# A weight rounding rewritten with an integer addition, and small sums, pooling and maxima moved, in a fused attention and mixing kernel

## The chip, the cores and the metric

One Trainium2 chip, one core. The metric is the device time of one execution in microseconds (us), median of three runs; lower is better.

## What is computed

For each of 8 batches and 8 heads: 1152 keys of width 64, and 576 queries that are the means of two neighbours. Then softmax attention, and a second stage on its output `x` (8 x 576 x 512):

```python
q_pool = q.reshape(B, H, S // 2, 2, D).mean(axis=3)
scores = scale * q_pool @ k.T ; scores -= scores.max(-1)
x = (exp(scores) / (exp(scores).sum(-1) + 1e-9)) @ v
theta = x @ w_theta
y = w_tok_r @ (x * cos(theta)) + w_tok_i @ (x * sin(theta))
u = x + y
out = u + max(u @ w_ch, 0)
```

q, k and v are 32-bit floats. The four weight matrices come as 64-bit floats, two 32-bit words each, and the kernel narrows them itself.

## The kernel before

**Stage one** takes the heads in 32 pairs. A pair has 18 steps, which the code calls positions: two halves `u` of the queries, with 9 key tiles `kt` each. In a step `escore` (line 671) issues four kinds of products on TensorE (high and low parts, and one that subtracts the row maximum), and ScalarE takes the exponential of the result into a buffer `pc` (line 674), of which there are 14. GpSimd adds the buffers of a half up, `ssum` (line 686): for each half seven additions of 128 x 576 numbers, key tiles 0 to 7 (`TAIL = 8`). The ninth tile, `kt = 8`, is not added there. `norm_sum` (line 735) sums over the keys with products by a block of ones, and takes the buffers from `TAIL` on as further operands. It runs a whole pair later, just after the first burst of the next pair, so that such a buffer is held until then. For pairs in `WHOLE` (25 to 30) VectorE adds the ninth tile instead (`whole_sum`, line 754).

A **burst** (`av`, line 706) is the product with v: 36 matmul instructions that read the nine `pc` buffers of one half. It stands at positions 10.348 (first half) and 19.269 (second half, so 1.269 of the next pair). ScalarE then copies the result (`xu`, line 718) and the row of maxima (line 629).

Meanwhile the next pairs are prepared: `load_q` and `load_k` by DMA, `pool_q` (line 487), which adds neighbouring queries, some 2.8 pairs ahead, on VectorE for pairs in `POOL_V` (before: none) and else on GpSimd; 32 x 32 transposes on VectorE (lines 516 and 520), rounding to the high part on ScalarE (`round_hi`, line 528), and the low part on VectorE (`round_lo`, line 572). TensorE also computes a rough product for the row maxima two pairs ahead (`maxpass`, line 585), which VectorE reduces (lines 597 and 616).

**Weights.** Beside this runs a generator, `weights`, with 18 jobs: four blocks each of `w_theta` and `w_ch` (128 x 512), five each of the two token matrices (128 x 576, the last 64 x 576). Each `yield` names the kind of the next step, and the table `W_SLOTS` says at which positions of a pair a step of a kind may run: F fetches the next block, A is work of ScalarE, D of VectorE, G of GpSimd, S and T split the result into high and low parts (T with transposes on TensorE). A job takes one pair. In the pairs of `REST` the slots after position 10.3455 are left out, so that those pairs do only the head of a job. `narrow` makes a 32-bit float from the two words: line 814 takes the absolute value of the high word, 815 scales the low word, 817 and 819 clamp and shift on VectorE, 824 puts the sign back, 828 masks the exponent, 830 multiplies it with the scaled low word on GpSimd, and 832 adds both there.

**Order.** The order of each engine's instructions is written out: every call goes on a list with a position and a priority (`at`, `plan`), which is then sorted; nothing is reordered afterwards. `PLAN`, `MAX_A`, `MAX_B` and `ROUND_AT` hold positions relative to the pair that is prepared; `SS_LAG` is how far an addition of line 686 stands behind its exponential.

```python
PC_BUFS = 14
at(base + KT * u + kt, 1, escore, i, u, kt)
at(base + KT * u + kt + (SS_LAG if i < NPAIR - 1 else 1.2), 8, ssum, i, u, kt)
at(base + (AV_AT if i else AV_AT0)[u], 4, burst, i, u)
```

**Stage two** (lines 1092, 1139 and 324 on TensorE) follows from about 865 us on and is not touched by the change.

Of the kernel before, what the change touches and what calls it, by code (L numbers as in the profile page):

```python
# [10 lines left out]
F32 = mybir.dt.float32  # L11
F32R = mybir.dt.float32r
U32 = mybir.dt.uint32
I32 = mybir.dt.int32
AF = mybir.ActivationFunctionType
ALU = mybir.AluOpType
AX = mybir.AxisListType

EPS = 1e-9
TAIL = 8  # L20
REST = (3, 6, 9, 12, 15, 18)
WHOLE = range(25, 31)
WARM = 16
AGAIN = ((3, 3, 3, 3, 3, 3, 3, 3, 3, 5, 3, 3), (3, 2, 1, 1, 1, 1, 1, 1, 1, 1, 1, 1))
PC_BUFS = 14
MAX_A = ((-23.79, -21.22, -20.37, -19.03, -18.14, -16.75), (-22.88, -21.22, -20.11, -19.13, -18.62, -17.88))
MAX_B = ((-14.28, -12.84, -11.93, -9.1, -7.7, -7.7), (-14.26, -12.84, -11.93, -9.1, -8.62, -7.7))
LATE = (4, 5, 10, 11, 16, 17, 21, 22, 23, 24, 26, 27)
G_FROM = 20
G_AT = 3.43  # L30
SS_LAG = 6.71
AV_AT = (10.348, 19.269)
AV_AT0 = (10.348, 19.269)
W_SLOTS = ((2.5139, 'F'), (2.5144, 'G'), (3.4324, 'G'), (10.3436, 'S'), (10.3441, 'G'), (10.3446, 'T'), (10.3451, 'A'), (11.0187, 'D'), (11.0192, 'D'), (14.1909, 'F'), (17.9513, 'D'), (17.9518, 'D'))
W_STORE = 14.5
W_SLOTS0 = ((12.6, "F"),)
POOL_V = ()
ROUND1 = (-21.9, -21.8, -21.7)
LOADV = (-58.9, 11)
TAIL_IN = (3, 2)  # L40
# [11 lines left out]
NM_AT = (0.2, 13)  # L52
ROW_AT = (0.7, 13)
PLAN = {
    "load_q": -67.965,
    "load_k": -51.9564,
    "pool_q": -50.015,
    "turn_q": -34.8283,
    "turn_k": -34.0064,
    "tail": -25.3624,  # L60
    "round_lo": -25.1995,
    "load_max": -7.6,
    "load_v": -6.3045,
    "max_nm": -7.69,
    "norm_spread": 29.0,
    "norm_store": 20.81,
}
MAN = ("PE", "Activation", "DVE", "Pool", "SP")
RING = 4
# [35 lines left out]
OT_LAST = "htmmr"  # L105
CH_LAST = ("mr", "mr", "mm", "mh")
CH_BANK = "mrmr"
ROUND_AT = (-26.599, -26.599, -25.976)
XN_LEAD = 7.918
XF_LAG = 0.627  # L110
XS_LAG = 0.27
TINY = 2.0**-15
MAGIC = 12582912.0
INV2PI = 1.0 / (2.0 * math.pi)
C1 = 6.28125
C2 = 2.0 * math.pi - C1
# [5 lines left out]
def pooled_attention_moe_kernel(  # L122
# [11 lines left out]
    nc = tc.nc  # L134
    P = 128
    B, H, S, D = k.shape
    SQ = S // 2
# [4 lines left out]
    KT = S // P  # L142
# [22 lines left out]
    magic = const.tile([P, 1], F32, name="magic")  # L165
    nc.vector.memset(magic, MAGIC)
    halfpi = const.tile([P, 1], F32, name="halfpi")
# [21 lines left out]
    def done(name):  # L189
        slots.append(held.pop(name))  # L190
# [138 lines left out]
    def chain(b, j):  # L329
# [16 lines left out]
        if b == 0 and j == 0:  # L346
            pools["kk"] = kk
        nc.scalar.activation(kk, th, AF.Identity, bias=magic, scale=INV2PI)
        yield
        nc.vector.tensor_scalar(kk, kk, -MAGIC, None, ALU.add)  # L350
        r2 = tmp("r2")
# [62 lines left out]
    with ExitStack() as p1:  # L414
# [67 lines left out]
        def pool_q(i):  # L482
            qn = state[i]["qn"]
            qp = state[i]["qp"] = inp.tile([P, TB, 32], F32, tag="qp", name=f"qp{i}")
            eng = nc.vector if i in POOL_V else nc.gpsimd
            a, b = (qn.rearrange("p (m x) r -> p m x r", x=2)[:, :, x] for x in range(2))
# [190 lines left out]
        def ssum(i, u, kt):  # L677
            st = state[i]
            if i == NPAIR - 1:
                return last_sum(st, u, kt)  # L680
            if kt == 0 or kt >= TAIL:
                return
            if kt == 1:
                st["ss", u] = nrm.tile([P, 2, HALF], F32, tag=f"ss{u}", name=f"ss{u}_{i}", bufs=2)
            first = st["pc"][u, 0] if kt == 1 else st["ss", u]
            nc.gpsimd.tensor_tensor(st["ss", u], first, st["pc"][u, kt], ALU.add)  # L686

        def last_sum(st, u, kt):
            if kt < 2 or kt >= TAIL:
                return  # L690
# [32 lines left out]
        def norm_sum(i, px):  # L723
            st = state[i]
            last = i == NPAIR - 1
            sets = [
                ([st["sum", u, 0], st["sum", u, 1]] if last else [st["ss", u]])
                + [st["pc"][u, kt] for kt in range(TAIL, KT) if i not in WHOLE]
                for u in range(2)
            ]  # L730
            for n in range(len(sets[0])):
                for h in range(2):
                    for u in range(2):
                        a = 32 * (2 * h + u)
                        nc.tensor.matmul(  # L735
                            px[a : a + 32, 1, 0:HALF],
                            ones,
                            sets[u][n][:, h, :],
                            start=(n == 0),
                            stop=(n == len(sets[0]) - 1),  # L740
                            tile_position=(0, a),
                        )
            sm = st["sm"] = sml.tile([P, HALF], F32, tag="sm", name=f"sm{i}", bufs=1)
            if last:
                nc.vector.tensor_scalar(sm, px[:, 1, 0:HALF], EPS, None, ALU.add)
            else:
                nc.scalar.activation(sm, px[:, 1, 0:HALF], AF.Identity, bias=eps)
            done("pend" if last else f"pn{i + 1}")

        def whole_sum(i, u):  # L750
            if i in WHOLE:
                st = state[i]
                for kt in range(TAIL, KT):
                    nc.vector.tensor_tensor(st["ss", u], st["ss", u], st["pc"][u, kt], ALU.add)
# [28 lines left out]
        def weights():  # L783
            wst = pw.enter_context(tc.tile_pool(name="wst", bufs=1, side="right"))
            wide = w_theta.dtype != F32

            def words(w):
                if not wide:
# [11 lines left out]
            def narrow(raw, ws, R, n, g):  # L800
                dst = ws[0:R, 0:n].rearrange("a (t p) -> a p t", t=g)
                if not wide:
                    yield "D"
                    nc.vector.tensor_copy(
                        dst, raw[0:R, 0:n, 0].rearrange("a (p t) -> a p t", t=g)
                    )
                    yield "F"
                    return
                lo, hi = raw[0:R, 0:n, 0], raw[0:R, 0:n, 1]
                f = wst.tile([P, SQ], U32, tag="wf", name="wf")[0:R, 0:n]  # L810
                tl = lo.bitcast(F32)
                mk = ws[0:R, 0:n]
                yield "A"
                nc.scalar.activation(mk, hi.bitcast(F32), AF.Abs)
                nc.scalar.activation(tl, lo, AF.Copy, scale=2.0**-52)
                yield "D"
                nc.vector.tensor_scalar(mk, mk, TINY, None, ALU.max)
                yield "D"
                nc.vector.tensor_scalar(
                    f, mk.bitcast(U32), 3, 0x3FFFFFF8, ALU.logical_shift_left, ALU.bitwise_and  # L820
                )
                yield "F"
                yield "D"
                nc.vector.scalar_tensor_tensor(
                    f, hi, 0xC0000000, f, ALU.bitwise_and, ALU.bitwise_or
                )
                yield "D"
                nc.vector.tensor_scalar(hi, f, 0xFF800000, None, ALU.bitwise_and)
                yield "G"
                nc.gpsimd.tensor_tensor(tl, tl, hi.bitcast(F32), ALU.mult)  # L830
                yield "G"
                nc.gpsimd.tensor_tensor(
                    dst,
                    f.bitcast(F32).rearrange("a (p t) -> a p t", t=g),
                    tl.rearrange("a (p t) -> a p t", t=g),
                    ALU.add,
                )

# [119 lines left out]
        def plan(i):  # L958
# [15 lines left out]
            for n, (prio, fn) in fns.items():  # L974
                if n in EARLY.get(i, ()):
                    at(EARLY[i][n], prio, fn, i)
                elif i > 2 and n in pl:
                    at(base + pl[n], prio, fn, i)
            for n, t in enumerate(ROUND_AT if i > 2 else ()):
                at(base + t, 3, round_hi, i, n)  # L980
# [15 lines left out]
            for n in (MAX_AT0, MAX_AT1, MAX_AT2)[i] if i < 3 else (  # L996
                MAX_A[i - 2 in LATE] + MAX_B[i - 2 in LATE]
            ):
# [3 lines left out]
            for u in range(2):  # L1002
                for kt in range(KT):
                    at(base + KT * u + kt, 1, escore, i, u, kt)
                    at(base + KT * u + kt + (SS_LAG if i < NPAIR - 1 else 1.2), 8, ssum, i, u, kt)
            for u in range(2):
# [25 lines left out]
        for j in range(AHEAD):  # L1032
            t = NU * (NPAIR - 1) + TH_AT[j]
# [6 lines left out]
        for i in range(NPAIR):  # L1040
            at(NU * i + W_STORE, 11, wstore)
            for pos, kinds in W_SLOTS if i else W_SLOTS0:
                if i in REST and pos > 10.3455:
                    continue
                at(NU * i + (G_AT if pos == 5.0 and i >= G_FROM else pos), 10, wstep, kinds)
        for _, _, _, fn, args in sorted(todo, key=lambda e: e[:3]):
            fn(*args)

    with ExitStack() as p2:
# [157 lines left out]
        for b in range(B):  # L1207
            base = CYC * b
            if b > 0:
# [4 lines left out]
                for c in range(ND):  # L1214
                    at2(DN1_AT[c] if b == 1 else base + DN_AT[c], dload, b, c)
                    t = SC1_AT + 0.01 * c if b == 1 else base + SC_AT[c]
# [12 lines left out]
            for n, j in enumerate(TURNS[b % 2] if b else TURN0):  # L1229
                t = base + (THETA_AT if b % 2 == 0 else ODD_THETA_AT)[n] if b else THETA0_AT[n]  # L1230
# [15 lines left out]
            for g in range(2):  # L1246
                for i in range(KW):
                    at2(base + TOK_AT[g][i], token_mix, b, g, i)
                for c in (2 * g, 2 * g + 1):
                    t = base + PLAN2[f"uadd{g}"] + 0.7 * (c - 2 * g)  # L1250
# [7 lines left out]
            t = base + CH_AT[0]  # L1258
# [53 lines left out]
```

## Time and profile before

| | us |
|---|---|
| median of three runs (1306.94 to 1308.79) | 1308.12 |
| the profiled execution, whole | 1309.01 |
| its span, first to last instruction | 1307.2 |
| TensorE busy | 1252.2 |
| VectorE busy | 979.7 |
| GpSimd busy | 934.5 |
| ScalarE busy | 682.4 |

The span is the part that the trace shows; 1.8 us of the execution lie around it. PE is TensorE's matmuls, PEld its weight loads, DVE VectorE, ACT ScalarE, POOL GpSimd, SP the engine that issues DMAs. Busy time of PE is modelled and overlaps from one matmul to the next, so the length of a stretch is read from start to start. The burst of pair 0 starts at 37.82 us, that of pair 1 at 66.45, and the last pair's at 846.99; a pair's period is counted from first burst to first burst.

### The profile page before, as it was taken

What the parts mean: (1) busy time and instruction counts of PE and PEld (TensorE: products, weight loads), DVE (VectorE), ACT (ScalarE), POOL (GpSimd) and SP (SyncE); (2) the same over time, 40 slices, a digit from 0 to 9 for tenths busy, and PEclk for the clock granted to TensorE, in tenths of its full rate; (3) what the DMA queues carried; (4) which work ended last, traced back from release to release, by engine and by line L of the source; (5) the groups of instructions that cost most, each with busy time, mean ns of one, the idle gap of its engine ahead of it and who ended that gap; (6) DMA issues with size and microseconds to landing.
All of it is one profiled execution on the core that took longest, in us unless ns stands there. A gap on an engine that the chain in (4) does not pass through costs nothing.

```text
span 1307.2 us, 28852 instructions
## 1 busy us (share of the span) xinstructions
PE 1252.2 (96%) x11404; PEld 1005.6 (77%) x11404; DVE 979.7 (75%) x1183; ACT 682.4 (52%) x1223; POOL 934.5 (71%) x635
## 2 busy tenths in 40 slices
PE   7999999999999999999999899998999999999998
PEld 5666676667677676766666677778999999999998
DVE  5798787968888697888897798666767668667652
ACT  3566476656656665666555465573344434434420
POOL 4799999999999999999999999741513234242420
PEclk8999999989999999999999899999999999999999
DMA  8645454545545544565445731024564554645421
GB/s 123 123 98 118 83 110 83 118 90 107 96 101 101 104 90 99 98 111 103 99 75 96 146 71 39 29 88 124 121 149 87 124 99 114 137 91 144 86 37 37
DMA packets 468659, 129.06 MB, mean 99 GB/s; under 512 B 438390, under 2 KB 438780, under 8 KB 468524
## 3 DMA queue, kind: packets, MB, share of 16 engines
q1 hardware_dynamic: 465728, 126.03, 47.7%
q8 instruction: 89, 1.46, 0.5%
q10 hardware_dynamic: 2572, 0.86, 0.3%
q14 instruction: 46, 0.38, 0.1%
q0 software_dynamic: 224, 0.33, 0.1%
HBM read 96.58 MB, written 29.55 MB: 96 GB/s over the span
## 4 chain that ended last, share of the span: by engine, by line
PE 60%; DVE 11%; POOL 11%; ACT 6%; DMA 5%; SPq 4%; issue 3%; ACTq 0%; POOLq 0%; DVEq 0%
PE pa L706 15%; PE pe L671 14%; PE pf L1092 14%; POOL ss L686 10%; PE pf L1139 5%; PE pf L324 5%; ACT pc L674 3%; PE pm L585 3%; DMA dn<-rd 2%; DVE mx L597 2%; DVE lo L572 2%; PE px L610 1%; SPq L461 1%; DMA kn<-in_k_dram 1%; PE pn L735 1%
## 5 line engine op out<-in xcount | busy, mean ns | idle before, releaser
L686 POOL TENSOR_TENSOR ss<-ss,pc 128x576 f32<-128x576 f32 x372 | 581.6, 1564 | 24.1 <-ACT pc L674 0.8
L597 DVE TENSOR_REDUCE mx<-pm 128x2 f32<-128x768 f32 x384 | 350.8, 951 | 109.8 <-PE pm L585 106.8
L674 ACT ACTIVATE pc<-pe 128x576 f32<-128x576 f32 x576 | 352.7, 651 | 112.7 <-PE pe L671 54.3
L706 PE MATMUL pa<-pc,vn 128*64 128x288 f32 x2304 | 299.5, 414 | 0.0
L706 PEld LDWEIGHTS pa<-pc,vn 128*64 128x64 f32 x2304 | 161.4, 139 | 119.9 <-issue 14.6
L1092 PE MATMUL pf<-wtk,Z 128*128 128x288 f32 x1728 | 234.0, 295 | 4.3 <-DVE Z L404 3.5
L1092 PEld LDWEIGHTS pf<-wtk,Z 128*128 128x128 f32 x1728 | 232.1, 189 | 6.0 <-DVE Z L404 3.7
L404 POOL TENSOR_TENSOR Z<-ab,Z 128x512 fp32r<-128x512 f32 x35 | 47.1, 1347 | 264.2 <-ACT Z L398 227.3
L671 PE MATMUL pe<-hi 64*128 64x288 f32 x1152 | 196.8, 337 | 14.9 <-ACT pc L674 8.8
L671 PE MATMUL pe<-nmr,oner 64*128 64x288 f32 x1152 | 171.8, 293 | 1.5 <-DMA nmr<-mT 1.5
L671 PE MATMUL pe<-hi,lo 64*128 64x288 f32 x1152 | 171.7, 294 | 0.0
L671 PE MATMUL pe<-lo,hi 64*128 64x288 f32 x1152 | 171.6, 294 | 0.0
L671 PEld LDWEIGHTS pe<-hi 64*128 64x128 f32 x1152 | 108.8, 185 | 71.8 <-ACT pc L674 22.6
L585 PE MATMUL pm<-hi 64*128 64x384 f32 x826 | 139.7, 356 | 10.6 <-DVE mx L597 7.5
L718 ACT COPY xu<-pa 128x288 f32<-128x288 f32 x64 | 25.5, 399 | 188.6 <-PE pa L706 141.7
L671 PEld LDWEIGHTS pe<-nmr,oner 64*128 64x128 f32 x1152 | 110.3, 186 | 2.1 <-DMA nmr<-mT 2.0
L671 PEld LDWEIGHTS pe<-lo,hi 64*128 64x128 f32 x1152 | 110.1, 187 | 0.0
L671 PEld LDWEIGHTS pe<-hi,lo 64*128 64x128 f32 x1152 | 109.8, 187 | 0.0
L1139 PEld LDWEIGHTS pf<-us,wch 128*128 128x128 f32 x768 | 104.0, 188 | 2.0 <-issue 0.5
L1139 PE MATMUL pf<-us,wch 128*128 128x288 f32 x768 | 105.4, 296 | 0.1
L686 POOL TENSOR_TENSOR ss<-pc,pc 128x576 f32<-128x576 f32 x62 | 104.1, 1679 | 0.0
L585 PEld LDWEIGHTS pm<-hi 64*128 64x128 f32 x826 | 79.2, 190 | 20.2 <-DVE mx L597 9.8
(163 smaller groups left out, 1554.8 us busy)
## 6 DMA issues: line engine op xcount, KB each, us to landing
vn<-in_v_dram SPq DMA_DIRECT2D x128, 144.0 KB
kn<-in_k_dram SPq DMA_DIRECT2D x124, 144.0 KB
qn<-in_q_dram SPq DMA_DIRECT2D x124, 144.0 KB
xd<-xu SPq DMA_DIRECT2D x32, 288.0 KB
xT<-xd SPq DMA_DIRECT2D x8, 1152.0 KB
out_dram<-ot SPq DMA_DIRECT2D x112, 72.0 KB
xn<-xs SPq DMA_DIRECT2D x31, 256.0 KB
dn<-rd SPq DMA_DIRECT2D x32, 160.0 KB
```

Source lines behind the costliest of these rows:

```text
L324: nc.tensor.matmul(th, xs[:, c, j * P : (j + 1) * P], ws[:, c], start=(n == 0), stop=(n == 11))
L404: eng.tensor_tensor(Z[1], t, Z[0].bitcast(F32), ALU.subtract)
L572: eng.tensor_tensor(lo, st["kb"][:, a:b], st["hi"][:, a:b].bitcast(F32), ALU.subtract)
L585: nc.tensor.matmul(pm[:, h, 0:W], hi[hs, Q0 + j * P : Q0 + (j + 1) * P], hi[hs, g * W : (g + 1) * W], start=True, stop=True,)
L597: nc.vector.tensor_reduce(mx[:, j : j + 5 : 4, g : g + 1], pm[:, :, 0:W], AX.X, ALU.max)
L671: nc.tensor.matmul(pe[:, h, 0:HALF], w[hs], x[hs], start=(n == 0), stop=(n == 3))
L674: nc.scalar.activation(pcs[u, kt], pe[:, :, 0:HALF], AF.Exp, scale=SC)
L686: nc.gpsimd.tensor_tensor(st["ss", u], first, st["pc"][u, kt], ALU.add)
L706: nc.tensor.matmul(pa[hs, 0, 0:HALF], st["vn"][:, h, kt, :], st["pc"][u, kt][:, h, :], start=(kt == 0), stop=(kt == KT - 1),)
L718: nc.scalar.copy(st["xu"][:, u, :], pa[:, 0, 0:HALF])
L1092: nc.tensor.matmul(st["py", c, u][:, 0:HALF], Z[zi][:, c * P : (c + 1) * P], wtk[wi][:, kw, u * HALF : (u + 1) * HALF], start=(i == 0 and ...
L1139: nc.tensor.matmul(st["pr", e][u][:, 0:HALF], wch[wi][:, c, e * P : (e + 1) * P], st["us", ui, c // 2][:, c % 2, u * HALF : (u + 1) * HALF ...
```

## The change

It does six things. Thirteen pairs (`SHORT`) stop the GpSimd additions one key tile earlier, at `kt = 6`, and give tile 7 to the product with ones too. `WHOLE` is empty, so that pairs 25 to 30 give tile 8 to that product as well. `POOL_V` sends ten `pool_q` to VectorE. In `narrow` the low word is rounded to an integer from 0 to 8 on ScalarE (three instructions where there were two), and GpSimd adds it to the float's bits as a 32-bit integer; the mask on VectorE and the multiplication on GpSimd go. The clamp and the shift now pass their data through a tile of three rows, each padded by one element. Positions of the maxima, the loads, the transposes, the roundings and the weight steps are changed.

```diff
+SHORT = (2, 3, 5, 7, 9, 11, 15, 16, 17, 21, 23, 28, 30)
-WHOLE = range(25, 31)
+WHOLE = ()
-MAX_A = ((-23.79, -21.22, -20.37, -19.03, -18.14, -16.75), (-22.88, -21.22, -20.11, -19.13, -18.62, -17.88))
-MAX_B = ((-14.28, -12.84, -11.93, -9.1, -7.7, -7.7), (-14.26, -12.84, -11.93, -9.1, -8.62, -7.7))
+MAX_A = ((-23.16, -21.04, -20.44, -19.56, -18.24, -16.98), (-23.16, -21.62, -20.02, -18.45, -18.24, -16.98))
+MAX_B = ((-14.02, -12.66, -11.75, -9.19, -7.7, -7.7), (-14.06, -12.34, -11.84, -9.56, -8.45, -7.73))
-SS_LAG = 6.71
+SS_LAG = 6.079
-W_SLOTS = ((2.5139, 'F'), (2.5144, 'G'), (3.4324, 'G'), (10.3436, 'S'), (10.3441, 'G'), (10.3446, 'T'), (10.3451, 'A'), (11.0187, 'D'), (11.0192, 'D'), (14.1909, 'F'), (17.9513, 'D'), (17.9518, 'D'))
+W_SLOTS = ((2.7077, 'F'), (2.7082, 'G'), (9.553, 'G'), (9.5535, 'S'), (10.1975, 'G'), (10.3446, 'T'), (10.3451, 'A'), (10.8111, 'D'), (10.975, 'D'), (19.0577, 'F'), (19.0582, 'D'), (19.0587, 'D'))
-POOL_V = ()
+POOL_V = (5, 6, 11, 13, 15, 19, 20, 22, 28, 31)
...
-    "load_q": -67.965,
-    "load_k": -51.9564,
-    "pool_q": -50.015,
-    "turn_q": -34.8283,
-    "turn_k": -34.0064,
-    "tail": -25.3624,
-    "round_lo": -25.1995,
+    "load_q": -68.4151,
+    "load_k": -51.0861,
+    "pool_q": -50.4651,
+    "turn_q": -35.8189,
+    "turn_k": -33.1361,
+    "tail": -25.0724,
+    "round_lo": -25.5568,
...
-    "load_v": -6.3045,
+    "load_v": -2.4391,
...
-    "norm_store": 20.81,
+    "norm_store": 21.2335,
...
-ROUND_AT = (-26.599, -26.599, -25.976)
+ROUND_AT = (-26.519, -26.42, -26.127)
...
-            if kt == 0 or kt >= TAIL:
+            if kt == 0 or kt >= TAIL - (i in SHORT):
...
-                + [st["pc"][u, kt] for kt in range(TAIL, KT) if i not in WHOLE]
+                + [st["pc"][u, kt] for kt in range(TAIL - (i in SHORT), KT) if i not in WHOLE]
...
-                f = wst.tile([P, SQ], U32, tag="wf", name="wf")[0:R, 0:n]
+                f = wst.tile([P, SQ + 3], U32, tag="wf", name="wf")
+                w = -(-n // 6) * 6
+                mg = f[0:R, 0 : w + 3].rearrange("a (o t) -> a o t", o=3)[:, :, 0 : w // 3]
+                mk = ws[0:R, 0:w].rearrange("a (o t) -> a o t", o=3)
+                f = f[0:R, 0:n]
                 tl = lo.bitcast(F32)
-                mk = ws[0:R, 0:n]
                 yield "A"
-                nc.scalar.activation(mk, hi.bitcast(F32), AF.Abs)
-                nc.scalar.activation(tl, lo, AF.Copy, scale=2.0**-52)
+                nc.scalar.activation(ws[0:R, 0:n], hi.bitcast(F32), AF.Abs)
+                nc.scalar.activation(tl, lo, AF.Identity, bias=big[0:R], scale=2.0**-29)
+                nc.scalar.activation(lo, tl, AF.Identity, bias=nbig[0:R])
                 yield "D"
-                nc.vector.tensor_scalar(mk, mk, TINY, None, ALU.max)
+                if w > n:
+                    nc.vector.memset(ws[0:R, n:w], 1.0)
+                nc.vector.tensor_scalar(mg.bitcast(F32), mk, TINY, None, ALU.max)
                 yield "D"
                 nc.vector.tensor_scalar(
-                    f, mk.bitcast(U32), 3, 0x3FFFFFF8, ALU.logical_shift_left, ALU.bitwise_and
+                    mk.bitcast(U32), mg, 3, 0x3FFFFFF8, ALU.logical_shift_left, ALU.bitwise_and
                 )
                 yield "F"
                 yield "D"
                 nc.vector.scalar_tensor_tensor(
-                    f, hi, 0xC0000000, f, ALU.bitwise_and, ALU.bitwise_or
+                    f, hi, 0xC0000000, ws[0:R, 0:n].bitcast(U32), ALU.bitwise_and, ALU.bitwise_or
                 )
-                yield "D"
-                nc.vector.tensor_scalar(hi, f, 0xFF800000, None, ALU.bitwise_and)
-                yield "G"
-                nc.gpsimd.tensor_tensor(tl, tl, hi.bitcast(F32), ALU.mult)
                 yield "G"
                 nc.gpsimd.tensor_tensor(
-                    dst,
-                    f.bitcast(F32).rearrange("a (p t) -> a p t", t=g),
-                    tl.rearrange("a (p t) -> a p t", t=g),
+                    dst.bitcast(U32),
+                    f.rearrange("a (p t) -> a p t", t=g),
+                    lo.rearrange("a (p t) -> a p t", t=g),
                     ALU.add,
                 )
```

## Rows read from the trace of the kernel before

**Rows 1.** The page: busy time of the engines, GpSimd in 40 slices, the chain.
```profile
PE 1252.2 (96%) x11404; PEld 1005.6 (77%) x11404; DVE 979.7 (75%) x1183; ACT 682.4 (52%) x1223; POOL 934.5 (71%) x635
...
POOL 4799999999999999999999999741513234242420
...
PE 60%; DVE 11%; POOL 11%; ACT 6%; DMA 5%; SPq 4%; issue 3%; ACTq 0%; POOLq 0%; DVEq 0%
```
**Rows 2.** Busy time by stretch (pairs 1-8, 9-16, 17-24, 25-30): PE, PEld, DVE, ACT, POOL, clock.
```profile
66.45:270.93 204.48, 197.88 (x2091) 143.36 (x2090) 172.47 (x174) 127.26 (x236) 198.83 (x132) 0.98 0.51 101
270.93:479.09 208.16, 200.55 (x2096) 144.60 (x2096) 167.69 (x172) 127.00 (x236) 202.28 (x135) 0.98 0.53 101
479.09:689.64 210.55, 199.05 (x2107) 143.34 (x2106) 180.23 (x185) 129.95 (x243) 204.90 (x136) 1.00 0.51 97
689.64:846.99 157.35, 150.10 (x1527) 110.17 (x1526) 122.06 (x120) 88.31 (x165) 145.67 (x92) 0.97 0.36 75
```
**Rows 3.** The same view for single pairs: 27, 12, 13, 10.
```profile
747.82:771.71 23.89, 23.80 (x254) 17.37 (x253) 22.00 (x22) 14.57 (x28) 23.03 (x16) 1.00 0.58 95
351.64:375.79 24.15, 24.04 (x262) 17.56 (x261) 16.66 (x21) 15.96 (x31) 23.29 (x17) 1.00 0.47 88
...
375.79:400.15 24.36, 24.10 (x262) 17.62 (x261) 22.96 (x23) 14.48 (x28) 23.65 (x16) 1.00 0.50 97
...
300.94:325.94 25.00, 24.92 (x267) 18.05 (x266) 23.23 (x24) 15.29 (x29) 24.37 (x17) 1.00 0.48 91
```
**Rows 4.** Waits of ACT from 66.45 to 846.99: total us, times, longest.
```profile
ACT xu L718 <- PE pa L706: 128.9, 30, 6.5
...
ACT pc L674 <- POOL ss L686: 40.4, 45, 2.0
```
**Rows 5.** Timeline of pair 15, ACT and PE, from 434 to 447.
```profile
438.04 0.65 ACT L674 ACTIVATE pc<-pe 128x576 f32<-128x576 f32 x1 [1.95 <-POOL ss L686]
...
438.75 0.49 PE L671 MATMUL pe<-hi 64*128 64x288 f32 x2 [1.62 <-ACT pc L674]
```
**Rows 6.** Groups of POOL instructions by line and shape: busy us, mean ns, idle before.
```profile
L686 POOL TENSOR_TENSOR ss<-ss,pc 128x576 f32<-128x576 f32 x372 | 581.6, 1564 | 24.1 <-ACT pc L674 0.8
...
L487 POOL TENSOR_TENSOR qp<-qn 128x576 f32<-128x576 f32 x31 | 44.6, 1437 | 24.3 <-DMA qn<-in_q_dram 24.3
...
L832 POOL TENSOR_TENSOR ws<-wf,raw 128x576 f32<-128x576 f32 x8 | 11.8, 1469 | 0.0
...
L830 POOL TENSOR_TENSOR raw<-raw 128x576 f32<-128x576 f32 x8 | 9.2, 1147 | 0.0
```
**Rows 7.** The same view for DVE.
```profile
L373 DVE TENSOR_TENSOR ab<-xn,ab 128x512 f32<-128x512 f32 x30 | 20.8, 692 | 47.4 <-ACT ab L368 39.0 <-issue 3.7 <-DMA xn<-xs 2.8
...
L754 DVE TENSOR_TENSOR ss<-ss,pc 128x576 f32<-128x576 f32 x12 | 16.6, 1381 | 0.0
...
L350 DVE TENSOR_SCALAR kk<-kk 128x512 f32<-128x512 f32 x36 | 16.3, 454 | 54.1 <-ACT kk L348 54.1
...
L817 DVE TENSOR_SCALAR ws<-ws 128x576 f32<-128x576 f32 x8 | 13.4, 1675 | 0.0
...
L828 DVE TENSOR_SCALAR raw<-wf 128x576 uint32<-128x576 uint32 x8 | 12.5, 1557 | 0.3
```
**Rows 8.** The same view for ACT: the scaling of the low word.
```profile
L815 ACT ACTIVATE raw<-raw 128x576 f32<-128x576 uint32 x8 | 6.0, 752 | 0.0
```
**Rows 9.** Timeline of pair 10: PE's burst, products with ones, next step; SP; ACT's wait.
```profile
300.94 4.59 PE L706 MATMUL pa<-pc,vn 128*64 128x288 f32 x36
...
306.12 0.67 PE L735 MATMUL pn<-pc,ones 128*32 128x288 f32 x8
306.72 0.40 PE L671 MATMUL pe<-hi 64*128 64x288 f32 x2
...
311.48 2.05 SPq L797 DMA_DIRECT2D raw<-in_moe_w_tok_i_dram  x4
...
305.72 0.40 ACT L718 COPY xu<-pa 128x288 f32<-128x288 f32 x1 [2.74 <-PE pa L625]
```

More of the change, by code (lines that the diff above doesn't have):

```diff
@@ L25 @@
 PC_BUFS = 14
-MAX_A = ((-23.79, -21.22, -20.37, -19.03, -18.14, -16.75), (-22.88, -21.22, -20.11, -19.13, -18.62, -17.88))
-MAX_B = ((-14.28, -12.84, -11.93, -9.1, -7.7, -7.7), (-14.26, -12.84, -11.93, -9.1, -8.62, -7.7))
+MAX_A = ((-23.16, -21.04, -20.44, -19.56, -18.24, -16.98), (-23.16, -21.62, -20.02, -18.45, -18.24, -16.98))
+MAX_B = ((-14.02, -12.66, -11.75, -9.19, -7.7, -7.7), (-14.06, -12.34, -11.84, -9.56, -8.45, -7.73))
 LATE = (4, 5, 10, 11, 16, 17, 21, 22, 23, 24, 26, 27)
 G_FROM = 20
-G_AT = 3.43
-SS_LAG = 6.71
+G_AT = 3.88
+SS_LAG = 6.079
 AV_AT = (10.348, 19.269)
 AV_AT0 = (10.348, 19.269)
-W_SLOTS = ((2.5139, 'F'), (2.5144, 'G'), (3.4324, 'G'), (10.3436, 'S'), (10.3441, 'G'), (10.3446, 'T'), (10.3451, 'A'), (11.0187, 'D'), (11.0192, 'D'), (14.1909, 'F'), (17.9513, 'D'), (17.9518, 'D'))
+W_SLOTS = ((2.7077, 'F'), (2.7082, 'G'), (9.553, 'G'), (9.5535, 'S'), (10.1975, 'G'), (10.3446, 'T'), (10.3451, 'A'), (10.8111, 'D'), (10.975, 'D'), (19.0577, 'F'), (19.0582, 'D'), (19.0587, 'D'))
 W_STORE = 14.5
 W_SLOTS0 = ((12.6, "F"),)
-POOL_V = ()
+POOL_V = (5, 6, 11, 13, 15, 19, 20, 22, 28, 31)
 ROUND1 = (-21.9, -21.8, -21.7)
@@ L113 @@
 MAGIC = 12582912.0
+BIG = 2.0**23
 INV2PI = 1.0 / (2.0 * math.pi)
@@ L785, in weights @@
             wide = w_theta.dtype != F32
+            big, nbig = (wst.tile([P, 1], F32, name=n) for n in ("big", "nbig"))
+            nc.vector.memset(big, BIG)
+            nc.vector.memset(nbig, -BIG)
             def words(w):
```

## The prediction

> **What bounds the kernel now.** I read the page first: TensorE is busy for 96% of the span, and it holds most of the chain that ended last [rows 1]. That points at TensorE, but the GpSimd line under it stands at nine tenths in almost every slice until about 800 us and falls after that [rows 1]. So there are two candidates in stage one. The view by stretch settles it in part: GpSimd is busy for 198.8, 202.3 and 204.9 us of 204.5, 208.2 and 210.6 us in pairs 1 to 24, which is 97% each time [rows 2]. What is left (17.2 us over 24 pairs, 0.7 us a pair) is the step from one instruction to the next.
>
> Single pairs show what TensorE can do when GpSimd doesn't hold it up. Pair 27, with one set of products with ones, took 23.89 us; pair 12, with two sets and no transposes of weights, 24.15; pair 13, with a weight job, 24.36; pair 10, with a token job and its transposes, 25.00 [rows 3]. The mean over pairs 1 to 24 is 623.2 / 24 = 25.97 us. TensorE's modelled busy time hides this difference, which is why I trust start-to-start periods.
>
> How GpSimd slows TensorE is seen in the waits: ScalarE waited 45 times, 40.4 us in all, for an addition of line 686 [rows 4]. It waits there for one of the 14 `pc` buffers. In pair 15 ScalarE stood 1.95 us, and TensorE, whose result it should have taken out, 1.62 us [rows 5]. [...]
>
> **The work that GpSimd loses in pairs 1 to 24.** Eleven of the thirteen SHORT pairs lie there (28 and 30 don't). Two additions each at 1.56 us [rows 6] are 22 x 1.56 = 34.4 us. Eight of the ten poolings run there (a pooling runs 2.8 pairs ahead of its own pair), 8 x 1.44 = 11.5 us [rows 6]. Eighteen multiplications at about 1.1 us [rows 6] are 19.8 us. Sum 65.7 us. GpSimd's busy time falls from 606.0 to 540.3 us, 22.5 us a pair, 23.2 with the steps between instructions.
>
> **The integer addition** has no row. Its nearest row is the float addition that it replaces, same operands, same strides, 1.47 us [rows 6]. The bounds I take are 1.15 us, the cheapest two-input instruction on GpSimd of this shape, and 2.62 us, which is the addition and the multiplication together (the change then saves nothing there) [rows 6]. I take 1.47: the data moved are the same. At 2.62 GpSimd needs 18 x 1.15 = 20.7 us more, 23.4 + 0.7 = 24.1 us a pair.
>
> **What TensorE gains in work.** One more set of products with ones is 8 instructions, 306.12 to 306.72: 0.60 us [rows 9]. SHORT adds it after 13 pairs (11 of them in pairs 1 to 24: 6.6 us), the empty WHOLE after 6 pairs.
>
> **The new period of pairs 1 to 24.** Ten pairs with a token job at 25.00, eight with another job at 24.36 and six in REST at 24.15 make 589.8 us, with the 6.6 us 596.4, or 24.8 a pair. This is above GpSimd's 23.2, so TensorE and its hand-over to ScalarE set the pace, and GpSimd catches up within a pair. Gain: 623.2 - 596.4 = 26.8 us.
>
> **Pairs 25 to 31.** Six pairs at 23.89 would be 143.3 us; they took 157.35 with GpSimd at 145.7, 93% [rows 2]. About a third of the excess of 14 us, 4.7 us, I put down to GpSimd (the rest is waits for loads of stage two, not touched). Against it stand 8 more sets (6 WHOLE, SHORT 28 and 30): 4.8 us. Net nothing; bounds -5 and +5.
>
> **VectorE** loses the mask, 18 x 1.56 = 28.0 us, and the additions of WHOLE, 12 x 1.38 = 16.6 us [rows 7]. It gains ten poolings. Nearest row: a two-input addition of that shape, 1.38 us beside a busy GpSimd [rows 7]; 10 x 1.38 = 13.8 us, and at least 0.69 each (the 512-wide product in stage two [rows 7]). In a weight pair VectorE was busy for 23.2 of 25.0 us [rows 3]; it now has room. Its gain lies beside TensorE's work, so I cost it at nothing; the small fills of four columns too.
>
> The clamp took 1.68 us here but an instruction of the same kind took 0.45 us in stage two, where GpSimd has little to do [rows 1, 7]: it is mostly waiting. The padded rows may make it an ordinary instruction that does not wait; bounds per instruction 0.69 (the 692 ns row, nearest in size) and 1.68 (as now) [rows 7]. I take the lower one, as the padded output can't be read as one run; it is no term of my sum.
>
> [...]
>
> **ScalarE** gains 18 x 0.75 = 13.5 us [rows 8]. It lies in front of the copies after a burst, where ScalarE waited 128.9 us in all for line 706 [rows 4], in pair 10 with its weight steps still 2.74 us [rows 9]. Without that cover it would cost its 13.5 us. The function of the new instructions is one that line 747 already uses among the exponentials.
>
> **Moved steps.** The fetch of the next block (four issues on SP, 2.05 us [rows 9]) now stands at 19.06 and is wanted at 28.35: 9.3 positions of 1.38 us (24.8 / 18), 12.8 us. On SP it is still behind the v load, and moves nearer the key and query loads, which are wanted over a pair later. The v load moves to 12.8 positions, 17 us, ahead of its burst. Loads, poolings and transposes move by up to a position, with their buffers handed over in the same order. I cost all of it at nothing. What is late next: TensorE's own products, and after a burst ScalarE's exponentials.
>
> **Sum.** 1309.0 (whole execution; span 1307.2 and 1.8 around it) - 26.8 = 1282.2; the median of the runs lies 0.9 lower than the profiled execution, so 1281.3, rounded to 1282.
>
> **Rivals.**
> *A: the SHORT pairs starve `pc` (slower).* Their four buffers (tiles 7 and 8 of both halves) are held until the products with ones a pair later. At the next pair's eleventh exponential, eleven buffers are its own; with two held that was 13 of 14, with four it is 15. If the free buffer is the first one that the burst has read, a ninth of 4.59 us in [rows 9], it waits 0.5 us, all under the burst. If the plan gives it one that the products with ones release, it waits past the burst, and in front of it stand, on ScalarE's queue, the weight step (3 x 0.75 = 2.25 us) and the exponential, 0.65 us, which would then run while TensorE waits: 2.9 us in 11 pairs, 0.65 in 2, 33 us. Time 1282 + 33 = 1315. Which buffer is taken decides. For it: only one buffer was spare. Against: TensorE works in order, and the burst releases before those products. 9%.
>
> *B: GpSimd stays the bound.* TensorE's 596.4 us less the 17.2 and the 540.3 leave 38.9 us, 2.2 us for each of 18 integer additions above the price taken. Above 3.6 us the addition sets the period; at 2.62, 24.1 of 24.8 us a pair is close enough that bad moments remain, and I give half the gain: 1282 + 13 = 1295. 14%.
>
> [...]
>
> *D: all rough places go.* With VectorE lighter, every pair at 24.15, sets included: 623.2 - 24 x 24.15 = 43.6 us; 1308.1 - 43.6 = 1264.5. For it: pair 12 did so. Against: pair 10's 25.00 had a saturated TensorE. 10%.
>
> **How the numbers follow.** The forecast has 50%; with C it makes 67% around 1278 to 1290. The range takes in B's 1295 and its slower bound, reaching 1301, and most of the way to D, 1267; outside are A and the far part of D, some 15 to 18%. About 0.2%, 2.6 us, is what a measurement of this kernel can tell from no change. Slower than that: most of A, 8%; within: the edges of A and B, 4%; faster: 88%.
>
> **What would show it.** Right: periods of pairs 1 to 24 near 24.8 us, GpSimd under 95% there, the waits of line 674 for line 686 down to a few us, and the clock 1.00 in the stretches of pairs 9 to 16. [...] I'm wrong if pairs without GpSimd waits still take 26 us, since then something else than these buffers held TensorE.

## The result and the profile after

The changed kernel took 1276.9 us (median of four executions; 1274.62 to 1278.34) against 1308.1 us before: a ratio of 0.9761, 95% interval 0.9744 to 0.9778. That is 31.2 us less, where 26 us were forecast; 1282 was predicted, with a range of 1267 to 1301. The profiled execution is the slowest of the four, 1278.34 us; its span is 1276.6 us.

Lines moved: 487 is now 489, 674 is 676, 686 is 688, 706 is 708, 718 is 720, 735 is 737, 585 and 597 are 587 and 599, 814 is 822, 815 is 823 and 824, 817 and 819 are 828 and 830, 832 is 839.

First the page of the changed kernel: busy time, GpSimd in 40 slices, and the chain by engine.

```profile
PE 1246.7 (98%) x11556; PEld 1006.2 (79%) x11556; DVE 903.5 (71%) x1173; ACT 696.2 (55%) x1241; POOL 854.1 (67%) x581
...
POOL 4799899899899979999998887432423514242410
...
PE 76%; DVE 5%; DMA 5%; POOL 4%; SPq 4%; ACT 3%; issue 3%; ACTq 0%; DVEq 0%; POOLq 0%
```

GpSimd's row of nines [rows 1] now has eights in it, and its share of the chain fell from 11% to 4%. The view by stretch, for the same four groups of pairs (columns: length, busy time of PE, PEld, DVE, ACT and POOL, granted clock, share of the DMA engines, GB/s):

```profile
68.85:265.00 196.15, 195.48 (x2124) 142.56 (x2123) 151.09 (x175) 132.12 (x242) 182.09 (x120) 1.00 0.58 110
265.00:461.50 196.50, 195.74 (x2120) 142.79 (x2120) 152.34 (x173) 130.56 (x240) 181.94 (x119) 1.00 0.56 106
461.50:659.63 198.13, 197.44 (x2138) 143.83 (x2138) 161.45 (x182) 135.41 (x250) 181.70 (x121) 1.00 0.56 103
659.63:813.33 153.70, 149.44 (x1575) 109.98 (x1573) 104.57 (x110) 87.53 (x164) 126.20 (x82) 0.99 0.36 76
```

Against [rows 2] the first three stretches lost 8.3, 11.7 and 12.4 us, 32.4 in all; the fourth 3.7. GpSimd is busy for 92 to 93% of them instead of 97%, and the clock is 1.00 in all three. The other parts of the span went the other way: the start up to the burst of pair 1 takes 68.85 us instead of 66.45, and from the last pair's burst on it is 463.3 us instead of 460.2 [rows 2 give the starts]. The sum, -32.4 - 3.7 + 2.4 + 3.1, is the -30.6 us between the spans. The last two of these are not shown to be the change's: in the runs below the burst of pair 1 starts between 66.57 and 70.32 us, and the part from the last pair's burst on, which none of them edits, takes 459.8 to 463.0 us.

The same view for single pairs, here 12, 13 and 10:

```profile
339.18:363.73 24.55, 24.50 (x269) 17.82 (x269) 16.88 (x21) 16.80 (x32) 22.45 (x16) 1.00 0.51 89
363.73:387.85 24.12, 24.00 (x262) 17.56 (x261) 18.94 (x23) 14.52 (x28) 22.28 (x15) 1.00 0.55 107
...
289.12:314.37 25.25, 25.21 (x275) 18.28 (x274) 20.23 (x23) 15.13 (x29) 22.55 (x15) 1.00 0.58 108
```

The pairs are now regular: 24.12 us plain (pair 13), 0.43 more after a SHORT pair (pair 12), and 25.25 with both a SHORT pair in front and a token job (pair 10). TensorE is busy through all of it and GpSimd is not. The waits of ScalarE from 68.85 to 813.33 us (total, times, longest) say the same:

```profile
ACT xu L720 <- PE pa L708: 141.3, 30, 4.8
...
ACT pc L676 <- POOL ss L688: 2.2, 9, 0.4
```

ScalarE's wait for a `pc` buffer went from 40.4 us [rows 4] to 2.2 us. Of the instructions that were disputed (groups by line and shape; busy us, mean ns, idle time before them), on GpSimd, VectorE and ScalarE:

```profile
L839 POOL TENSOR_TENSOR ws<-wf,raw 128x576 uint32<-128x576 uint32 x8 | 11.5, 1438 | 7.9 <-DVE wf L835 5.5 <-DMA raw<-in_moe_w_tok_i_dram 1.3 <-DMA raw<-in_moe_w_theta_dram 1.1
...
L489 DVE TENSOR_TENSOR qp<-qn 128x576 f32<-128x576 f32 x10 | 10.6, 1057 | 0.0
...
L828 DVE TENSOR_SCALAR wf<-ws 128x576 f32<-128x576 f32 x8 | 5.9, 741 | 0.0
...
L823 ACT ACTIVATE raw<-raw,big 128x576 f32<-128x576 uint32 x8 | 6.7, 837 | 0.0
```

The integer addition takes 1.44 us, as the float one did [rows 6]; the padded clamp 0.74 us instead of 1.68 [rows 7].

### The profile page after: what moved, and what is told of

Same layout as the page of the kernel before. It is cut to its first block, busy times and chain, and to the rows that moved or that the text cites. A ratio compares the mean times of both kernels' runs of the same rounds, so it can differ in the third digit from the quotient of the medians.

```text
span 1276.6 us, 29050 instructions
## 1 busy us (share of the span) xinstructions
PE 1246.7 (98%) x11556; PEld 1006.2 (79%) x11556; DVE 903.5 (71%) x1173; ACT 696.2 (55%) x1241; POOL 854.1 (67%) x581
## 4 chain that ended last, share of the span: by engine, by line
PE 76%; DVE 5%; DMA 5%; POOL 4%; SPq 4%; ACT 3%; issue 3%; ACTq 0%; DVEq 0%; POOLq 0%
PE pe L673 22%; PE pa L708 20%; PE pf L1099 13%; PE pf L1146 5%; PE pf L326 5%; PE pm L587 4%; POOL ss L688 4%; PE pn L737 3%; ACT pc L676 2%; DMA dn<-rd 2%; PE px L612 2%; SPq L463 1%; DVE xT L250 1%; SPq L1207 1%; DMA xs<-dn 1%
## 5 line engine op out<-in xcount | busy, mean ns | idle before, releaser
L688 POOL TENSOR_TENSOR ss<-ss,pc 128x576 f32<-128x576 f32 x346 | 531.2, 1535 | 50.4 <-ACT pc L676 27.8
L708 PE MATMUL pa<-pc,vn 128*64 128x288 f32 x2304 | 294.4, 409 | 0.0
L587 PE MATMUL pm<-hi 64*128 64x384 f32 x826 | 134.5, 349 | 4.7 <-ACT hi L558 1.6
L688 POOL TENSOR_TENSOR ss<-pc,pc 128x576 f32<-128x576 f32 x62 | 100.7, 1624 | 0.4 <-ACT pc L676 0.4
```

The costliest lines, as they stand in the source:

```text
L587: nc.tensor.matmul(pm[:, h, 0:W], hi[hs, Q0 + j * P : Q0 + (j + 1) * P], hi[hs, g * W : (g + 1) * W], start=True, stop=True,)
L708: nc.tensor.matmul(pa[hs, 0, 0:HALF], st["vn"][:, h, kt, :], st["pc"][u, kt][:, h, :], start=(kt == 0), stop=(kt == KT - 1),)
```

## The experiments

Theory 1 says that GpSimd's work set the pace of pairs 1 to 24, and that a part of the change is worth the GpSimd time it takes away, until TensorE's own pace is reached. Theory 2 says that the new order of the work is the gain, theory 3 that it is the new rounding in all its parts. "Before" was run beside each group: 1308.6, 1309.0 and 1308.5 us.

**Positions alone.** The diff against the changed kernel; the old `narrow` is the one of the diff above:

```diff
-SHORT = (2, 3, 5, 7, 9, 11, 15, 16, 17, 21, 23, 28, 30)
+SHORT = ()
-WHOLE = ()
+WHOLE = range(25, 31)
-POOL_V = (5, 6, 11, 13, 15, 19, 20, 22, 28, 31)
+POOL_V = ()
 narrow: as before
```

> The changed positions with the old rounding, the additions of line 686 up to tile 7 in every pair, the VectorE additions in pairs 25 to 30 and all pooling on GpSimd: only the order of the work changes against the kernel before. Theory 1 (GpSimd's work set the pace): GpSimd has the same instructions, so the time stays near before, 1303 to 1310 us, with ScalarE's waits for line 686 near 40 us. Theory 2 (the new order of maxima, roundings and loads is the gain): 1280 to 1288 us.

It took 1338.0 us, ratio 1.0228 (1.0206 to 1.0250): slower than before by 29 us, which neither theory foresaw. Its waits of PE during the pairs have one that the kernel before does not have, and the timeline of POOL and PE around one token job shows where it comes from (line 834 here is the old line 832, line 876 T's transposes):

```profile
PE pwt L876 <- POOL ws L834: 29.9, 10, 4.9
```
```profile
170.31 2.88 POOL L688 TENSOR_TENSOR ss<-ss,pc 128x576 f32<-128x576 f32 x2
173.14 1.43 POOL L834 TENSOR_TENSOR ws<-wf,raw 128x576 f32<-128x576 f32 x1
...
169.46 0.33 PE L596 MATMUL pm<-hi,tail 128*128 128x128 f32 x1
174.62 1.12 PE L876 MATMUL pwt<-ident,ws 128*128 128x128 f32 x4 [4.84 <-POOL ws L834]
```

The old rounding has two GpSimd steps. In the new table the second falls to 9.553 instead of 3.4324, here right behind the two additions of the first row, and T's transposes stand at 10.3446. TensorE stood 4.84 us for it here and 29.9 us in all. So the new positions are no gain by themselves; they fit the shorter job.

**The new work at the old positions.** `MAX_A`, `MAX_B`, `SS_LAG`, `W_SLOTS`, `PLAN`, `ROUND_AT` as before, all else as changed.

> The changed kernel with all positions (maxima, plan, roundings, weight steps, the lag of the additions) set back to those of before; the work moved off GpSimd stays off. Theory 1: GpSimd is at about 93% as in the changed kernel, so most of the gain stays: 1278 to 1286 us. Theory 2: 1300 to 1310 us.

1283.7 us, ratio 0.9806 (0.9783 to 0.9828). Theory 2 falls: 25 of the 31 us are there without any new position. The remaining 7 us are the positions'; which of them, no run shows. Its row for pairs 1 to 24 has 9.1 us more than the changed kernel's 590.8, with GpSimd equally light:

```profile
67.27:667.15 599.88, 593.16 (x6380) 429.60 (x6379) 460.85 (x528) 401.00 (x730) 543.35 (x358) 1.00 0.56 104
```

**The new rounding alone, at the old positions.**

```diff
-SHORT = (2, 3, 5, 7, 9, 11, 15, 16, 17, 21, 23, 28, 30)
+SHORT = ()
-WHOLE = ()
+WHOLE = range(25, 31)
-POOL_V = (5, 6, 11, 13, 15, 19, 20, 22, 28, 31)
+POOL_V = ()
 all positions: as before
```

> The kernel before with the new rounding alone: no SHORT pairs, VectorE additions in pairs 25 to 30, all pooling on GpSimd, all positions of before. Theory 1 (GpSimd's work set the pace): GpSimd loses the 18 multiplications, 19.8 us, and some waits: 1283 to 1291 us. Theory 3 (the rounding is nearly the whole gain, by VectorE's mask and the waits between the two engines as well): 1276 to 1281 us.

1288.4 us, ratio 0.9839 (0.9824 to 0.9854): inside theory 1's numbers, outside theory 3's. Its row for pairs 1 to 24 and ScalarE's wait:

```profile
67.85:670.43 602.58, 589.08 (x6292) 427.43 (x6291) 463.28 (x519) 399.70 (x730) 584.00 (x384) 1.00 0.54 103
```
```profile
ACT pc L676 <- POOL ss L688: 30.4, 45, 1.4
```

GpSimd is busy for 584.0 of 602.6 us, 97% as before: it still sets the pace, only with 22 us less to do than the 606.0 of [rows 2], and the pairs got 20.6 us shorter. ScalarE still waits for it.

**The moved row sums alone, at the old positions.** SHORT and the empty WHOLE as changed, `POOL_V = ()`, `narrow` and all positions as before.

> The kernel before with the row sums moved alone (SHORT, and WHOLE empty): old rounding, all pooling on GpSimd, all positions of before. Theory 1: GpSimd loses 34.4 us in pairs 1 to 24 and TensorE gains 4.7 us there and 3 us later: 1281 to 1290 us. Theory 3: 1300 to 1309 us.

1285.5 us, ratio 0.9824 (0.9799 to 0.9849): again theory 1's. In pairs 1 to 24:

```profile
66.85:667.97 601.12, 592.68 (x6379) 429.80 (x6379) 508.13 (x529) 383.70 (x712) 575.96 (x382) 1.00 0.55 102
```

Rounding alone gives 20.5 us and sums alone 23.5; both, with pooling, give 25 at the same positions. They don't add up, since each takes away the same bottleneck. This run also answers whether it was VectorE that held the pairs up: its load hardly changed here (508.1 us, 520.4 in [rows 2]), GpSimd's fell from 606.0 to 576.0 us, and the pairs got 22.1 us shorter.

**No SHORT pairs.**

```diff
-SHORT = (2, 3, 5, 7, 9, 11, 15, 16, 17, 21, 23, 28, 30)
+SHORT = ()
```

> The changed kernel with no SHORT pairs: 26 additions go back to GpSimd and 13 sets of products with ones leave TensorE. Theory 1: in pairs 1 to 24 GpSimd's busy time goes from 545.7 to 579.5 us (22 x 1.535), with 17 us of steps between instructions 596.5, which is more than TensorE's 590.8 less 11 x 0.43, so GpSimd sets the pace again: 1283 to 1290 us. Theory 2 (GpSimd does not matter): 13 x 0.43 us less on TensorE, 1271 us.

1277.9 us, ratio 0.9763 (0.9744 to 0.9782): no difference from the changed kernel, and in neither theory's range. Both effects are in its profile. GpSimd is busy for 575.4 of 594.7 us in pairs 1 to 24, 97% again, but these are only 3.9 us longer than in the changed kernel. Pair 3 takes 24.11 us, without the set of products that makes it 24.57; pair 15, with GpSimd busy for 26.70 of its 27.64 us, ran at a mean clock of 0.94, where pair 3 has 1.00:

```profile
411.72:439.36 27.64, 25.75 (x262) 18.20 (x261) 18.48 (x20) 17.30 (x32) 26.70 (x19) 0.94 0.64 114
116.06:140.17 24.11, 24.00 (x261) 17.58 (x260) 16.33 (x19) 17.29 (x32) 23.32 (x17) 1.00 0.49 103
```
```profile
ACT pc L676 <- POOL ss L688: 16.5, 22, 1.7
```

With the other parts in place the SHORT pairs pay back what they cost, no more.

**The old rounding at the new positions**, first with the new table of weight steps, then with the old `W_SLOTS`. The only edits are `narrow` and, in the second, the table.

> The changed kernel with the rounding of before (mask on VectorE, multiplication and float addition on GpSimd, clamp and shift unpadded), at the changed positions, whose table has a place for each of its steps. Theory 1: GpSimd goes from 545.7 to about 566 us in pairs 1 to 24, 583 with the steps between, still under 590.8: 1277 to 1284 us, the more the less evenly the extra steps fall. Theory 3 (the rounding is where the gain is, by the mask and by waits between VectorE and GpSimd): 1290 us or more.

> The changed kernel with the rounding of before and also its table of places for the weight steps; all else as changed. In the run with the old rounding at the new places, TensorE's transposes and ScalarE's splits came right behind GpSimd's second step and waited for it. Theory 1 (the places did that, not the work): 1278 to 1286 us. Theory 3 (the work did it): 1300 us or more.

1307.0 us (0.9985, 0.9973 to 0.9996) and 1289.3 us (0.9848, 0.9833 to 0.9862). The first lies in theory 3's range, the second in neither. The first has the wait of the positions-alone run (on this line 11.1 us), and the two differ by the table alone, so 18 us of its loss are the table's. In the second, 12 us remain, and its wait rows of PE name another engine; for the changed kernel the same row reads 3.6 us, once:

```profile
PE pe L673 <- DVE mx L599: 14.5, 13, 3.2
```

TensorE waits for maxima, which VectorE makes. VectorE is busy for 522.8 of 604.4 us in pairs 1 to 24 against 464.9 of 590.8 in the changed kernel. Three runs put back one piece of the old rounding each.

**Unpadded rows**, and one mask or one multiplication more in each weight job; nothing uses the two extra results:

```diff
-                mg = f[0:R, 0 : w + 3].rearrange("a (o t) -> a o t", o=3)[:, :, 0 : w // 3]
+                mg = f[0:R, 0:w].rearrange("a (o t) -> a o t", o=3)
...
+                nc.vector.tensor_scalar(hi, f, 0xFF800000, None, ALU.bitwise_and)
...
+                nc.gpsimd.tensor_tensor(hi.bitcast(F32), tl, hi.bitcast(F32), ALU.mult)
```

> The changed kernel with three rows that are not padded, so that the clamp and the shift can be read as one run. If the padding is what makes them short: 1.5 to 1.7 us each instead of 0.74, some 30 us more on VectorE in all, of which by theory 1 up to 5 us come through, 1277 to 1282 us. If it does nothing: 0.74 us each and 1277 us.

> The changed kernel with one mask more on VectorE in each weight job, as the old rounding had it; its result is used by nothing. VectorE +28 us. If VectorE has room (489 of 591 us): 1276 to 1280 us. If the VectorE part of the old rounding, its maxima coming later, is what cost 12 us with its old places: 1281 to 1288 us.

> The changed kernel with one multiplication more on GpSimd in each weight job, on the words that the old one read, in front of the integer addition; its result is used by nothing. GpSimd +20 us. Theory 1 (582 us with the steps between instructions, under 590.8): 1276 to 1280 us. If the GpSimd part of the old rounding is what cost 12 us with its old places: 1284 to 1290 us.

1277.8 us (0.9762, 0.9747 to 0.9776), 1276.3 us (0.9750, 0.9735 to 0.9765) and 1276.3 us (0.9751, 0.9734 to 0.9767): none differs from the changed kernel. The unpadded clamp and shift did get longer, by 22 us in pairs 1 to 24 (487.1 instead of 464.9 us of VectorE), and those pairs took only 2.7 us longer, less than the executions of the changed kernel differ:

```profile
L828 DVE TENSOR_SCALAR wf<-ws 128x576 f32<-128x576 f32 x8 | 9.7, 1211 | 0.0
...
L830 DVE TENSOR_SCALAR ws<-wf 128x576 uint32<-128x576 uint32 x8 | 11.3, 1409 | 0.3
```

So the padding shortens both (to 0.74 and 0.75 us at 128 x 576), and VectorE had the room. The extra mask came cheaper than the 28 us that were expected: 13.3 us in pairs 1 to 24 (478.2 instead of 464.9 us of VectorE). The extra multiplication brought GpSimd to 561.5 of 591.5 us, still without effect.

So no piece makes the 12 us by itself, at the price that it had here. That VectorE's load makes them is not shown either, and one run speaks against it: in the moved row sums alone the old rounding ran with all positions as before, VectorE was busy for 508.1 of 601.1 us, and the same row of TensorE's waits reads

```profile
PE pe L673 <- DVE mx L599: 2.5, 5, 0.6
```

Against the run with the new rounding at the same positions that one is only 1.8 us slower (1285.5 and 1283.7 us, whose intervals overlap; they differ in the pooling too). The 12 us therefore come with the old rounding and its old table among the other new positions. Which places clash there stays open; no run has the new rounding with the old table alone.

**All pooling on GpSimd** (`POOL_V = ()`).

> The changed kernel with all pooling on GpSimd. Theory 1: GpSimd from 550.3 to 561.7 us in pairs 1 to 24, 574 with the steps between instructions, under TensorE's 590.8: 1276 to 1280 us. If GpSimd is near its limit in the pairs with weight steps: 1281 to 1288 us.

1275.7 us, ratio 0.9746 (0.9731 to 0.9760): as theory 1 has it (GpSimd is busy for 555.4 us in pairs 1 to 24). The ten poolings on VectorE are not needed here.

**A version made from this**: no SHORT pairs, and GpSimd relieved by VectorE instead, which costs TensorE nothing.

```diff
-SHORT = (2, 3, 5, 7, 9, 11, 15, 16, 17, 21, 23, 28, 30)
+SHORT = ()
-POOL_V = (5, 6, 11, 13, 15, 19, 20, 22, 28, 31)
+POOL_V = tuple(range(4, 32))
```

> The changed kernel with no SHORT pairs, and instead the pooling of every pair from 4 on at VectorE (28 instead of 10). TensorE has 13 sets of products less, GpSimd 26 additions more and 18 poolings less, VectorE 18 poolings more. By theory 1 the GpSimd time in pairs 1 to 24 is 582.2 (without SHORT) less 16 x 1.42 = 559.5, 571 with the steps between instructions, under TensorE's 586; VectorE rises from 496 to about 513: 1270 to 1274 us, faster than the changed kernel. If VectorE's lateness counts as it did with the old rounding: 1276 to 1284 us.

1271.3 us, ratio 0.9718 (0.9704 to 0.9733), its slowest execution (1273.3) under the fastest of the changed kernel (1274.6). Pairs 1 to 24:

```profile
70.32:657.23 586.91, 583.42 (x6292) 426.22 (x6291) 475.17 (x543) 397.38 (x730) 563.71 (x361) 1.00 0.58 106
```

586.9 us is TensorE's pace without the extra sets (590.8 less 11 x 0.43 = 586.1). GpSimd, at 563.7 us, is under it, and VectorE at 475.2 too. The expectation started from 582.2 us of GpSimd and 496 of VectorE; the views by stretch have 575.4 (no SHORT pairs) and 464.9 (changed kernel).

## Why the prediction was right

**The bound.** GpSimd was read as the engine that set pairs 1 to 24, against the page's 96% for TensorE. The rounding-alone run shows it directly: GpSimd again at 97%, and the pairs shorter by about what it lost; with the moved row sums alone they got 22.1 us shorter with VectorE nearly as loaded as before. Its busy time after the change was forecast as 540.3 us and is 545.7. The clock is 1.00 in pairs 9 to 16, as forecast, where it was 0.98 before [rows 2].

**The integer addition** was taken at 1.47 us between 1.15 and 2.62, and is 1.44.

**TensorE's pace** was the term of the sum that was mis-sized. The floors I read off single pairs of before still held some waiting: 24.36 for a pair with a weight job is 24.12, 25.00 with a token job is 24.82 (25.25 less 0.43), and a set of products with ones is 0.43 instead of 0.60. I had measured that set to the start of the next step, which included the hand-over: in pair 3 of the changed kernel two sets take 1.09 us to the next step, not twice 0.60. So pairs 1 to 24 take 590.8 instead of 596.4 us: 3.7 us by the floors, 1.9 by the sets. That is a little more than the whole miss of 5 us.

**Pairs 25 to 31** were costed at nothing. Pairs 25 to 30 gained 3.7 us; what follows, last pair and stage two, lost 3.1 and the start 2.4, which the prediction did not have. That these nearly cancel is luck; the latter two are of the size by which the runs scatter.

**VectorE's gain** was costed at nothing. That holds for each piece by itself (mask, padding, pooling), and, with the row sums moved, for the whole rounding at the old positions (1.8 us). Only with the old table among the other new positions did 12 us return, TensorE waiting 14.5 us for maxima. That a term for VectorE's room was missing is not shown.

**Moved steps** were costed at nothing and are worth 7 us with the new work, which the sum has no term for; with the old work they lose 29. I had looked at what each position comes before, but not at whether a second GpSimd step of a job would land in front of TensorE's transposes.

**ScalarE's cover** held, with nothing over. In pair 3 of the changed kernel (timeline of ACT) the copy starts as the weight step ends, 0.2 us after the end of the burst (117.11 + 4.59 = 121.70):

```profile
119.06 0.64 ACT L676 ACTIVATE pc<-pe 128x576 f32<-128x576 f32 x1
119.60 0.75 ACT L822 ACTIVATE ws<-raw 128x576 f32<-128x576 f32 x1
120.25 0.83 ACT L823 ACTIVATE raw<-raw,big 128x576 f32<-128x576 uint32 x1
121.11 0.83 ACT L824 ACTIVATE raw<-raw,nbig 128x576 uint32<-128x576 f32 x1
121.89 0.40 ACT L720 COPY xu<-pa 128x288 f32<-128x288 f32 x1
```

**The rivals.** The first line of that timeline is also the answer to A: pair 2 is SHORT, the burst of pair 3 starts at 117.11, and the eleventh exponential starts 1.95 us later, inside the burst. The products with ones come after 121.78, so it got a buffer that the burst had released. B falls with GpSimd at 92 to 93% and the addition at 1.44 us. D was too hopeful: the token jobs keep their 0.7 us.

C was that the clamp stays near its old 1.68 us. It falls too: the clamp is 0.74 us, and 1.21 without the padding. I had taken the lower bound, 0.69 us. The runs show the times: three padded rows are shorter than three unpadded ones, 0.74 against 1.21 us for the clamp and 0.75 against 1.41 for the shift. That the old clamp was mostly waiting was my estimate from the 0.45 us in stage two [rows 7]; what in the padded shape shortens it, no run shows.

## What to carry to other kernels

Two engines can both look full; take the stretches where one has less to do, read the other's pace there from start to start, and the difference is the most that relief can bring. Relief of one engine is worth its time only down to the next engine's pace, so parts of such a change don't add up (20.5 and 23.5 us alone here, 25 together with the pooling), and one that pays with time of the next engine (here SHORT, on TensorE) should be tried without. Written-out positions belong to the work they were made for: a step more in a job can put a whole wait in front of another engine, and a part put back among positions that were not made for it shows that wait beside its own work.

## What was not expected of the hardware

An integer addition of 128 x 576 words on GpSimd cost here what the float addition did (1.44 and 1.47 us; at 128 x 512 it is 1.42 and 1.31 us, and 1.29 us at the shortest). A padded tile of three rows between the clamp and the shift made both shorter on VectorE beside a busy GpSimd, 0.74 and 0.75 instead of 1.2 to 1.4 us, although the same kind of instruction took 0.45 us unpadded at 128 x 512 in stage two [rows 7]. The ScalarE instructions with a bias tile took 0.84 and 0.85 us, where the plain scaling took 0.75 [rows 8].
